# Block-sparse attention and a rational FFN on one core: the first batch's keys stay in SBUF for all its parts, and GpSimd copies the sampled blocks

## The chip, the cores and the metric

One core of a Trainium2 chip runs the whole program. The metric is device time in microseconds (us) of one launch. Inputs come from the chip's memory (DRAM in the code) and the output goes back there. The engines are TensorE (PE in the profile), VectorE (DVE), ScalarE (ACT), GpSimd (POOL) and SyncE (SP), which issues nearly all DMA transfers. Each engine works through its own queue in order.

## The reference

Shapes: `q`, `k`, `v` are 4 batches x 8 heads x 768 positions x 64, in float32. Positions form 24 blocks of 32. `sampled_blocks` names three key blocks for each query block.

```
scores = scale * q @ k^T
mask: |query block - key block| <= 1, or either block is 0 or 23,
      or the key block is one of the three sampled for the query block
attn = softmax(where(mask, scores, -1e9)); attn_out = attn @ v
x = attn_out as 3072 tokens x 512
h = x @ w_in                          (512 x 2048)
P = a0 + a1 h + a2 h^2 + a3 h^3;  Q = 1 + |b0||h| + |b1| h^2
out = (P / (Q + 1e-6)) @ w_out        (2048 x 512)
```

`w_in` and `w_out` arrive as 64-bit floats, and the kernel unpacks them itself.

## The kernel before

**Attention.** The work is cut into parts, a query block of 32 rows each with all eight heads. An ordinary query block needs eight key blocks: itself and its two neighbours, three sampled ones (3 to 5 in the tile) and blocks 0 and 23 (6 and 7). Query blocks 0 and 23 need all 24 key blocks and are cut into three parts of eight (`n` is 3 for those, 1 otherwise). A batch thus has 22 + 6 = 28 parts, in the order that `block(j)` gives: blocks 1 to 11, block 0, blocks 12 to 22, block 23. A part goes through scores (TensorE, L869), maxima with a bias that masks doubled blocks (VectorE, L879), the exponentials (ScalarE, L892), transposes (L935), a copy of these to SBUF, and the product with the values in tile `vg` (L992), which come from DRAM for each part.

**Keys.** `prep` loads a batch's keys, finds a scale, splits them into f16 high and low halves and transposes them. For batch 0 the transposed keys land in `kall`, which holds all 24 blocks (12 KB in each partition). For later batches they land in `kt` and are stored to a DRAM tile `ks`. From `ks` each part loads its eight key blocks into a slot: one transfer for the neighbours, at times one for blocks 0 and 23 (`fresh`), and one for each sampled block, at a row that SP reads from the table `ix` into registers (`sampled_rows`, L768).

**The near parts.** Batch 0's keys are also stored to `ks`. Its first eight parts (`near`, `x < KX`, `KX = CB = 8`) use `kall` itself: VectorE reads the sampled rows into its registers and copies the three blocks to `kx`, and the scores take three pieces: neighbours (96 columns), `kx` (96), blocks 0 and 23 (64). All other parts of batch 0 load from `ks` like those of later batches. Their slots are the three thirds of `kall`, which become free when the near parts are done with it.

**FFN.** Tokens are cut into 12 chunks of 256 (three to a batch), and each chunk into eight units of 256 hidden columns: matmuls with `w_in` in high and low halves (L1090 to L1092), the rational function on ScalarE and VectorE, and matmuls with `w_out` (L1146 to L1148). Ahead of that, weights are loaded to `wl`, unpacked by VectorE (L434, L437, L440), and split by ScalarE and GpSimd: `w_in` through the two buffers `ws`, `w_out` through the two buffers `dw`. Early in the program the attention of batch 0, the preparation of batch 1, this unpacking and the first units run interleaved.

**The order.** Each piece of work is an `Op` with an engine, a price in ns, a priority `prio`, and the ring slots that it takes and uses. `issue` is a planner: it simulates the engines with these prices (a transfer costs its issue, 650 ns, its bytes at 360 bytes per ns, and 900 ns), and repeatedly emits the operation that can start first, priority deciding ties. The emitted order is then fixed in each engine's queue. Until its own clock reaches 80 us, the planner also emits dummy matmuls (`fill`, L159) where TensorE would be idle. So a change of an operation's engine or price can move later work to other places in the queues, too.

**The pool switch.** The tiles of `early` (weight unpacking, `kx`) are freed at one point (`switch`), after the last weight is unpacked, the last `kx` copy and the first chunk's input. Their memory then serves four more `ld` buffers and a fourth key slot, `xkg`.

Of the kernel before, what the change touches and what calls it, by code (L numbers as in the profile page):

```python
# [11 lines left out]
F32 = mybir.dt.float32  # L12
F32R = mybir.dt.float32r
F16 = mybir.dt.float16
I32 = mybir.dt.int32
# [8 lines left out]
def kernel(  # L24
# [27 lines left out]
    nc = tc.nc  # L52
    B, H, S, D = q.shape
    DM, DFF = out.shape[1], w_out.shape[0]
    P = 128
    BLK = 32
    NB = S // BLK
# [215 lines left out]
    r_ld, r_hl, r_kt = Ring([p3] * 3), Ring([None] * 2), Ring([None])  # L273
    r_ldq, r_hlq, r_qa, r_fc, r_ks = Ring([None]), Ring([None]), Ring([None] * 2), Ring([None] * 2), Ring([None] * 2)
    r_cq, r_scq, r_xn = Ring([None] * 4), Ring([None] * 3), Ring([None])
    r_wl, r_dw, r_ws, r_kx, r_sums = Ring([None] * 2), Ring([None] * 2), Ring([None] * 2), Ring([None] * 2), Ring([None] * 2)


    sb32 = sampled_blocks.bitcast(I32).rearrange("(o i) n -> o (i n)", o=1)
# [107 lines left out]
    WC = 512  # L387
# [13 lines left out]
    def weights():  # L401

        wi64, wo64 = w_in.bitcast(I32), w_out.bitcast(I32)
        pieces = []
        for u in range(NG):
            pieces += [(min(place[0, 2 * u], place[1, 2 * u]) + -4.91, 0, u, x) for x in range(NCC)]
        for x in range(NF):
            pieces.append((min(place[0, x // 2], place[1, x // 2]) + x % 2 / 2 + 0.45, 1, x // NCC, x))  # L410
        pieces.sort(key=lambda p: p[0])
        sums, before = {}, None

        def one(prio, kind, u, x, before):
            d = {}
            s_wl = Slot(r_wl)
            s_w = Slot(r_dw) if kind else None

            def load():
                d["ld"] = early.tile([P, 2 * WC], I32, name="wl", bufs=2)  # L420
                if kind:
                    nc.sync.dma_start(out=d["ld"], in_=wo64[x * P:(x + 1) * P])
                    return
                for g in range(2):
                    nc.sync.dma_start(out=d["ld"][g * D:(g + 1) * D], in_=wi64[(g * HG + x) * D:(g * HG + x + 1) * D, u * 2 * WC:(u + 1) * 2 * WC])

            def convert(eng):
                d["w"] = early.tile([P, WC], I32, name="dw") if kind else wi[:, x, u].rearrange("p a n -> p (a n)").bitcast(I32)
                d["words"] = d["ld"].rearrange("p (n w) -> p n w", w=2)
                times(eng, d["w"].bitcast(F32), d["words"][:, :, 1].bitcast(F32), 2.0 ** -112)  # L430

            def pack1():
                w = d["w"]
                nc.vector.tensor_scalar(out=w, in0=w, scalar1=3, scalar2=None, op0=ALU.logical_shift_left)  # L434

            def pack2():
                nc.vector.scalar_tensor_tensor(out=d["w"], in0=d["words"][:, :, 0], scalar=29, in1=d["w"], op0=ALU.logical_shift_right, op1=ALU.bitwise_or)  # L437

            def pack3():
                nc.vector.scalar_tensor_tensor(out=d["w"], in0=d["words"][:, :, 1], scalar=-2 ** 31, in1=d["w"], op0=ALU.bitwise_and, op1=ALU.bitwise_or)  # L440

            def most():
                if u not in sums:
                    sums[u] = early.tile([P, 8], F32, name="sums")
                bound(d["w"].bitcast(F32), sums[u][:, x:x + 1])

            def out_high(eng):
                times(eng, wo_h[:, x], d["w"].bitcast(F32), 1.0)

            def out_low(eng):  # L450
                eng.tensor_tensor(out=wo_l[:, x], in0=d["w"].bitcast(F32), in1=wo_h[:, x].bitcast(F32), op=ALU.subtract)  # L451

            o0 = Op(SY, [(475, 524288)] if kind else [(475, 262144)] * 2, load, (), prio - 2, takes=[s_wl], behind=before)
            w = [s_w] if kind else []
            o = Op(among("c", SC, sc=520, po=588, ve=335), 0, convert, [o0], prio, takes=w, uses=[s_wl])
            o = Op(VE, 335, pack1, [o], prio, uses=w)
            o = Op(VE, 602, pack2, [o], prio, uses=[s_wl] + w)
            o = Op(VE, 602, pack3, [o], prio, uses=[s_wl] + w)
            if kind:
                o1 = Op(among("o", SC, sc=520, po=588, ve=335), 0, out_high, [o], prio, uses=w)  # L460
                o2 = Op(among("p", PO, po=1225, ve=602), 0, out_low, [o1], prio, uses=w)
                out_ready[x] = [o2]
                decoded.append(o2)
                return o0, o2
            return o0, Op(SC, 613, most, [o], prio)

        group = []
        for prio, kind, u, x in pieces:
            before, o = one(prio, kind, u, x, before)
            if kind == 0:  # L470
                group.append(o)
                if x == NCC - 1:
                    group = w_scaled(u, prio, group, sums) or []

    def w_scaled(u, prio, group, sums):
# [9 lines left out]
        scale_ready[u] = o  # L485
        for x in range(NCC):
            def three(x):
                d, s_ws = {}, Slot(r_ws)

                def scaled(eng):  # L490
                    d["w"] = early.tile([P, WC], F32, name="ws")
                    times(eng, d["w"], wi[:, x, u].rearrange("p a n -> p (a n)").bitcast(F32), sc[0])

                def high(eng):
                    times(eng, wi[:, x, u, 0], d["w"], 1.0)

                def low(eng):
                    eng.tensor_tensor(out=wi[:, x, u, 1], in0=d["w"], in1=wi[:, x, u, 0], op=ALU.subtract)

                a = Op(among("s", PO, po=671, ve=396, sc=613), 0, scaled, [o], prio, takes=[s_ws])  # L500
                a = Op(among("h", SC, sc=520, po=588, ve=335), 0, high, [a], prio, uses=[s_ws])
                a = Op(among("l", PO, po=1113, ve=602), 0, low, [a], prio, uses=[s_ws])
                in_ready.setdefault(u, []).append(a)
                decoded.append(a)
            three(x)
# [109 lines left out]
    def rest(b, w, j, d, o_scale, sc, prio, before):  # L615
# [63 lines left out]
        a.behind = k_evac[b, t][0] if g else None  # L679
        c = Op(among("e", VE if on_dve[1] else SC, sc=478, ve=598), 0, evac(1), [o, a], prio, uses=[s_ps, sk])  # L680
        k_evac.setdefault((b, t), []).extend([a, c])
        if g == 1:
            k_done[b].append(Op(SY, [(475, 524288)], store, k_evac[b, t], prio + (13.03 if first else 0), uses=[sk, s_scr[b]]))

    k_evac = {}

# [93 lines left out]
        has[kind, slot.buf] = b if n == 1 else None  # L780
        return old != b

    KX = CB

    def v_plain(buf):

# [8 lines left out]
    def attention(b, j, prio):  # L795
# [11 lines left out]
        for m, x in enumerate(xs):  # L807
            def one(m, x):
# [3 lines left out]
                deps = [Q["oq"], Q["oc"]]  # L812
                kslots = []
                h = {}
                if near:
                    s_kx = Slot(r_kx)

                    def copies():
                        rows = sampled_rows(x, mybir.EngineType.DVE)
                        h["kx"] = early.tile([P, NR, H, BLK], F16, name="kx")  # L820
                        for r in range(NR):
                            o_, i_ = h["kx"][:, r].rearrange("p h r -> p (h r)"), kall[:, bass.ds(rows[r], 1)].rearrange("p o h r -> p (o h r)")
                            nc.vector.tensor_copy(out=o_, in_=i_)

                    a = Op(VE, 470, copies, [o_setup] + [o for t in range(NCH) for o in k_evac[b, t]], p - 1, takes=[s_kx], uses=s_kall)
                    deps.append(a)
                    kslots = [s_kx] + s_kall
                    last_copies.append(a)
                else:
                    s_kg = Slot(r_kg)  # L830

# [25 lines left out]
                def scores():  # L857
                    qa, qc = Q["q"]
                    h["sp"] = sp = ps_s.tile([P, 512], F32, name="sp").rearrange("p (g n) -> p g n", g=2)
                    spv = sp.rearrange("p g (s r) -> p g s r", r=BLK)  # L860
                    if near:
                        pieces = [(slice(0, 3), kall[:, i - 1:i + 2]), (slice(3, 3 + NR), h["kx"]), (slice(3 + NR, NS), kall[:, 0:NB:NB - 1])]
                    else:
                        pieces = [(slice(0, NS), kgs[s_kg.buf])]
                    for g in range(2):
# [9 lines left out]
                def maxima():  # L875
                    st = d["st"]
                    add = bias[:, i] if n == 1 else bias[:, 0, 0:1].broadcast_to([P, NS])
                    for g in range(2):
# [2 lines left out]
                            in1=add.rearrange("p (s o) -> p s o", o=1).broadcast_to([P, NS, BLK]),  # L881
                            op0=ALU.add, op1=ALU.max, scale=1.0, scalar=-3.0e38, accum_out=st[:, 2 * m + g:2 * m + g + 1])

                o = chain["sc"] = Op(TE, 1010 if near else 668, scores, deps, p, behind=chain.get("sc"), takes=[s_sp, s_pr] + ([s_st] if m == 0 else []),
                                     uses=kslots + [Q["slot"]] + ([] if m == 0 else [s_st]))
                o.work = 0.4 if near else 1.0
                omax.append(Op(VE, 690, maxima, [o, o_setup], p, uses=[s_sp, s_pr, s_st]))

                def exps():
# [158 lines left out]
        l = Op(VE, 602, evac_low, [a], p, uses=[s_ps, s_xs[c]])  # L1048
        o_ready.setdefault(c, []).append(l)

    last_copies = []
    XB = 4
    x_group = {}

# [176 lines left out]
        return lambda w, stage, j: p0 - A[stage] + (w * 6 + j) * (([0.5, 0.5] if b == 1 else [0.85, 0.83])[stage])  # L1231

    prep(0, when(0))
    weights()
    before = None
    for b in range(B):
# [17 lines left out]
    def switch():  # L1254
        early_cm.__exit__(None, None, None)
        ext.append(ctx.enter_context(tc.tile_pool(name="ext", bufs=1)))
        t = max(o.end for o in decoded)
        r_ld.free += [(t, ext[0])] * 4
        for j in range(1):
            kgs.append(ext[0].tile([P, NS, H, BLK], F16, name=f"xkg{j}"))  # L1260
            r_kg.free.append((t, len(kgs) - 1))

    Op(None, 0, switch, decoded + last_copies + o_ready[0], -1)
    ctx.enter_context(tc.manual_schedule(engines={getattr(mybir.EngineType, n) for n in (TE, SC, VE, PO, SY)}))
    issue(8)

# [28 lines left out]
```

## Time and profile before

| | |
|---|---|
| median of 3 runs | 916.02 us (915.13 to 920.15) |
| the profiled execution | 923.66 us, its span 921.9 us |
| TensorE, VectorE, ScalarE, GpSimd busy | 836.3, 760.6, 649.5, 125.2 us |
| mean granted TensorE clock | 0.959 |
| DMA traffic | 159.04 MB in 261124 packets, mean 173 GB/s |

The span runs from the first to the last instruction of one execution taken by the profiler. "Busy" is the time in which an engine executes. A row of the forty slices has one digit for each 23 us, the busy share in tenths. In a table of stretches, the columns are the limits, the length, each engine's busy time with its count of instructions, the granted clock, the mean share in which the 16 DMA engines were busy, and GB/s. A row of waits names who waited for whom, the total, how often, and the longest. A row of transfers gives the destination and source, the queue, the count, the size of each and the median time from issue to landing. A row of a timeline has start, duration, engine, line, operation and, in brackets, idle time ahead of it.

### The profile page before, as it was taken

What the parts mean: (1) busy time and instruction counts of PE and PEld (TensorE: products, weight loads), DVE (VectorE), ACT (ScalarE), POOL (GpSimd) and SP (SyncE); (2) the same over time, 40 slices, a digit from 0 to 9 for tenths busy, and PEclk for the clock granted to TensorE, in tenths of its full rate; (3) what the DMA queues carried; (4) which work ended last, traced back from release to release, by engine and by line L of the source; (5) the groups of instructions that cost most, each with busy time, mean ns of one, the idle gap of its engine ahead of it and who ended that gap; (6) DMA issues with size and microseconds to landing.
All of it is one profiled execution on the core that took longest, in us unless ns stands there. A gap on an engine that the chain in (4) does not pass through costs nothing.

```text
span 921.9 us, 27328 instructions
## 1 busy us (share of the span) xinstructions
PE 836.3 (91%) x10214; PEld 646.7 (70%) x10214; DVE 760.6 (83%) x2065; ACT 649.5 (70%) x1373; POOL 125.2 (14%) x125
## 2 busy tenths in 40 slices
PE   7798876578889989989999999989999999999997
PEld 3365554356668768768888777768877787788886
DVE  5667986899999778787888788779878988877886
ACT  6476664776868677768776788687777777767663
POOL 2123621345420000020000000110000000000000
PEclk9988997789999999999999999999999999999999
DMA  8889899999875896677756976677656566541000
GB/s 221 199 182 237 210 230 205 199 227 248 243 178 151 216 252 172 162 175 196 191 145 175 226 211 167 162 195 204 161 142 171 145 170 166 157 113 47 1 24 23
DMA packets 261124, 159.04 MB, mean 173 GB/s; under 512 B 17152, under 2 KB 245376, under 8 KB 260992
## 3 DMA queue, kind: packets, MB, share of 16 engines
q1 hardware_dynamic: 260992, 157.30, 68.4%
q8 instruction: 81, 1.33, 0.6%
q14 instruction: 51, 0.42, 0.2%
HBM read 138.36 MB, written 12.58 MB: 164 GB/s over the span
## 4 chain that ended last, share of the span: by engine, by line
PE 56%; DMA 13%; DVE 12%; SPq 5%; issue 4%; ACT 4%; POOL 1%; DVEq 0%; ACTq 0%; POOLq 0%
PE acc L1146 7%; PE ph L1090 7%; PE acc L1148 7%; PE acc L1147 7%; PE ph L1091 6%; PE ph L1092 6%; PE av L992 5%; PE sp L869 4%; PE pt L935 4%; DMA vg<-in_v_dram 3%; DMA ld<-in_k_dram 2%; DMA ldq<-in_q_dram 2%; DMA wl<-in_moe_w_in_dram 2%; DMA ks<-kt 1%; DMA kall<-ks 1%
## 5 line engine op out<-in xcount | busy, mean ns | idle before, releaser
L1090 PE MATMUL ph<-xh,wi 128*128 128x256 f16 x768 | 212.8, 277 | 2.0 <-DVE tt L1107 2.0
L1091 PE MATMUL ph<-xl,wi 128*128 128x256 f16 x768 | 211.5, 275 | 0.0
L1092 PE MATMUL ph<-xh,wi 128*128 128x256 f16 x768 | 211.3, 275 | 0.0
L1146 PE MATMUL acc<-wo_h,gh 128*128 128x512 f32 x384 | 164.2, 428 | 3.8 <-ACT ld L147 2.5
L1148 PE MATMUL acc<-wo_h,gl 128*128 128x512 f32 x384 | 154.3, 402 | 4.8 <-DVE gl L1135 4.8
L892 ACT ACTIVATE pr<-pr,st,cq 128x256 f32<-128x256 f32 x224 | 132.1, 593 | 36.3 <-DVE st L903 36.2
L1147 PE MATMUL acc<-wo_l,gh 128*128 128x512 f32 x384 | 153.7, 400 | 1.1 <-POOL wo_l L451 1.1
L1097 ACT ACTIVATE sq<-ph,fc 128x512 f32<-128x512 f32 x96 | 65.5, 682 | 77.8 <-PE ph L1092 77.6
L1114 DVE SCALAR_TENSOR_TENSOR ab<-sq,absb,ab 128x512 f32<-128x512 f32 x96 | 73.4, 765 | 35.9 <-ACT ab L1111 35.6
L1090 PEld LDWEIGHTS <-wi 128*128 128x128 f16 x768 | 76.0, 99 | 31.1 <-issue 18.3
L879 DVE CUSTOM_DVE_ANT_1 pr<-sp,bias 128x256 f32<-128x256 f32 x224 | 84.8, 418 | 14.7 <-PE sp L869 14.2
L992 PE MATMUL av<-vg,pT 128*32 128x64 f32 x3584 | 76.1, 228 | 21.8 <-DMA vg<-in_v_dram 14.3
L992 PEld LDWEIGHTS av<-vg,pT 128*32 128x32 f32 x3584 | 58.2, 113 | 48.4 <-issue 16.7
L1148 PEld LDWEIGHTS acc<-wo_h,gl 128*128 128x128 f32 x384 | 73.5, 191 | 24.1 <-DVE gl L1135 6.5
L151 POOL TENSOR_SCALAR hlq<-ldq,scq 128x512 f16<-128x512 f32 x24 | 24.4, 1016 | 481.9 <-DVE scq L352 292.2
L1146 PEld LDWEIGHTS acc<-wo_h,gh 128*128 128x128 f32 x384 | 73.5, 191 | 21.4 <-ACT ld L147 3.0
L935 PE MATMUL pt<-ident,pr 128*128 128x128 f32 x448 | 78.6, 297 | 8.3 <-ACT pr L892 7.7
L1147 PEld LDWEIGHTS acc<-wo_l,gh 128*128 128x128 f32 x384 | 73.8, 192 | 13.9 <-POOL wo_l L451 1.4
L1092 PEld LDWEIGHTS <-wi 128*128 128x128 f16 x768 | 75.9, 99 | 9.5
L1091 PEld LDWEIGHTS <-wi 128*128 128x128 f16 x768 | 76.0, 99 | 9.2 <-issue 1.2
L1125 DVE SCALAR_TENSOR_TENSOR gh<-tt,par,rr 128x512 fp32r<-128x512 f32 x96 | 74.5, 776 | 8.5 <-PE acc L1147 7.1
L935 PEld LDWEIGHTS pt<-ident,pr 128*128 128x128 f32 x448 | 67.1, 207 | 20.0 <-ACT pr L892 10.4
(138 smaller groups left out, 1663.7 us busy)
## 6 DMA issues: line engine op xcount, KB each, us to landing
vg<-in_v_dram SPq DMA_DIRECT2D x312, 64.0 KB, 3.3
vg<-in_v_dram SPq DMA_DIRECT2D x88, 192.0 KB, 4.2
vg<-in_v_dram SPq DMA_DIRECT2D x24, 512.0 KB, 4.8
kall<-ks SPq DMA_DIRECT2D x63, 192.0 KB, 3.7
kall<-ks SPq DMA_DIRECT2D x189, 64.0 KB, 2.5
kall<-ks SPq DMA_DIRECT2D x21, 512.0 KB, 6.3
ld<-in_k_dram SPq DMA_DIRECT2D x36, 256.0 KB, 5.4
wl<-in_moe_w_in_dram SPq DMA_DIRECT2D x32, 256.0 KB, 4.5
```

The lines of the kernel that those rows point to most:

```text
L879: nc.vector.tensor_tensor_reduce(out=prs[x][:, g].rearrange("p (s r) -> p s r", r=BLK), in0=h["sp"][:, g].rearrange("p (s r) -> p s r", r= ...
L892: nc.scalar.activation(out=prs[x][:, g], in_=prs[x][:, g], func=AF.Exp, scale=Q["c"], bias=st[:, 6 + g:7 + g], accum_out=st[:, 8 + 2 * m + ...
L935: nc.tensor.transpose(pp[:, jj * P:(jj + 1) * P], cols, ident)
L992: nc.tensor.matmul(av[rows, g], pT[:, 2 * g + kt, rows] if plain else pT[:, 2 * g + kt, pa_, rows], vf[:, g * HG + h4, kt * D:(kt + 1) * D ...
L1090: nc.tensor.matmul(o, wh, xh[:, :, cc], start=(cc == 0), stop=False)
L1091: nc.tensor.matmul(o, wh, xl[:, :, cc], start=False, stop=False)
L1092: nc.tensor.matmul(o, wl, xh[:, :, cc], start=False, stop=(cc == NCC - 1))
L1114: nc.vector.scalar_tensor_tensor(out=d["ab"], in0=d["sq"], scalar=absb[:, 1:2], in1=d["ab"], op0=ALU.mult, op1=ALU.add)
L1125: nc.vector.scalar_tensor_tensor(out=d["gh"], in0=d["tt"], scalar=par[:, 0:1], in1=d["rr"], op0=ALU.add, op1=ALU.mult)
L1146: nc.tensor.matmul(acc[:, t], ghs, wo_h[:, f], start=(new and e == 0), stop=False)
L1147: nc.tensor.matmul(acc[:, t], ghs, wo_l[:, f], start=False, stop=False)
L1148: nc.tensor.matmul(acc[:, t], gls, wo_h[:, f], start=False, stop=(last and e == 1))
```

## The change

All 28 parts of batch 0 are now near (`KX` counts them), and batch 0's keys are no longer stored to `ks` nor loaded from it. The six parts with `n > 1` use the thirds of `kall` as they are, in one piece, without a copy. For the 22 others GpSimd reads the sampled rows into its registers and copies the three blocks into one of the two buffers of a fixed tile, `kxs`. That tile also holds blocks 0 and 23, which GpSimd copies once into each buffer (`edges`), so that the scores take two pieces (96 and 160 columns). The rings of `ws` and `dw` become one of three buffers. The pool switch waits for the last near scores in place of the last copy and the first chunk's input.

```
-    r_wl, r_dw, r_ws, r_kx, r_sums = Ring([None] * 2), Ring([None] * 2), Ring([None] * 2), Ring([None] * 2), Ring([None] * 2)
+    r_wl, r_dw, r_kx, r_sums = Ring([None] * 2), Ring([None] * 3), Ring(range(2)), Ring([None] * 2)
...
-                d["w"] = early.tile([P, WC], I32, name="dw") if kind else ...
+                d["w"] = early.tile([P, WC], I32, name="dw", bufs=3) if kind else ...
...
-                d, s_ws = {}, Slot(r_ws)
+                d, s_ws = {}, Slot(r_dw)
...
-                    d["w"] = early.tile([P, WC], F32, name="ws")
+                    d["w"] = early.tile([P, WC], I32, name="dw", bufs=3).bitcast(F32)
...
-        if g == 1:
-            k_done[b].append(Op(SY, [(475, 524288)], store, k_evac[b, t], prio + (13.03 if first else 0), uses=[sk, s_scr[b]]))
+        if g == 1 and not first:
+            k_done[b].append(Op(SY, [(475, 524288)], store, k_evac[b, t], prio, uses=[sk, s_scr[b]]))
...
-    KX = CB
+    KX = sum(1 for p in parts if p[0] == 0)
+    kxs = early.tile([P, 2, NR + 2, H, BLK], F16, name="kx", bufs=1)
...
-                if near:
+                if near and n > 1:
+                    deps += [o for t in range(NCH) for o in k_evac[b, t]]
+                    kslots = s_kall
+                elif near:
                     s_kx = Slot(r_kx)
 
                     def copies():
-                        rows = sampled_rows(x, mybir.EngineType.DVE)
-                        h["kx"] = early.tile([P, NR, H, BLK], F16, name="kx")
+                        rows = sampled_rows(x, mybir.EngineType.Pool)
                         for r in range(NR):
-                            o_, i_ = h["kx"][:, r]..., kall[:, bass.ds(rows[r], 1)]...
-                            nc.vector.tensor_copy(out=o_, in_=i_)
-
-                    a = Op(VE, 470, copies, [o_setup] + [o for t in range(NCH) for o in k_evac[b, t]], p - 1, takes=[s_kx], uses=s_kall)
+                            nc.gpsimd.tensor_copy(out=kxs[:, s_kx.buf, r]..., in_=kall[:, bass.ds(rows[r], 1)]...)
+
+                    a = Op(PO, 1500, copies, [o_setup, chain["edges"]], p - 1, takes=[s_kx], uses=s_kall)
                     deps.append(a)
                     kslots = [s_kx] + s_kall
-                    last_copies.append(a)
...
-                    if near:
-                        pieces = [(slice(0, 3), kall[:, i - 1:i + 2]), (slice(3, 3 + NR), h["kx"]), (slice(3 + NR, NS), kall[:, 0:NB:NB - 1])]
+                    if near and n > 1:
+                        pieces = [(slice(0, NS), kgs[m])]
+                    elif near:
+                        pieces = [(slice(0, 3), kall[:, i - 1:i + 2]), (slice(3, NS), kxs[:, s_kx.buf])]
...
-                o = chain["sc"] = Op(TE, 1010 if near else 668, scores, ...
+                o = chain["sc"] = Op(TE, 800 if near else 668, scores, ...
...
+                if near:
+                    last_near.append(o)
...
+    def edges():
+        for e in range(2):
+            nc.gpsimd.tensor_copy(out=kxs[:, e, NR:]..., in_=kall[:, 0:NB:NB - 1]...)
...
+    chain["edges"] = Op(PO, 1400, edges, [o for t in range(NCH) for o in k_evac[0, t]], -40, uses=s_kall)
...
-        t = max(o.end for o in decoded)
+        t = max(o.end for o in decoded + last_near)
...
-    Op(None, 0, switch, decoded + last_copies + o_ready[0], -1)
+    Op(None, 0, switch, decoded + last_near, -1)
```

More of the change, by code (lines that the diff above doesn't have):

```diff
@@ L427, in convert @@
             def convert(eng):
-                d["w"] = early.tile([P, WC], I32, name="dw") if kind else wi[:, x, u].rearrange("p a n -> p (a n)").bitcast(I32)
+                d["w"] = early.tile([P, WC], I32, name="dw", bufs=3) if kind else wi[:, x, u].rearrange("p a n -> p (a n)").bitcast(I32)
                 d["words"] = d["ld"].rearrange("p (n w) -> p n w", w=2)
@@ L814, in one @@
                 h = {}
-                if near:
+                if near and n > 1:
+                    deps += [o for t in range(NCH) for o in k_evac[b, t]]
+                    kslots = s_kall
+                elif near:
                     s_kx = Slot(r_kx)
                     def copies():
-                        rows = sampled_rows(x, mybir.EngineType.DVE)
-                        h["kx"] = early.tile([P, NR, H, BLK], F16, name="kx")
+                        rows = sampled_rows(x, mybir.EngineType.Pool)
                         for r in range(NR):
-                            o_, i_ = h["kx"][:, r].rearrange("p h r -> p (h r)"), kall[:, bass.ds(rows[r], 1)].rearrange("p o h r -> p (o h r)")
-                            nc.vector.tensor_copy(out=o_, in_=i_)
-                    a = Op(VE, 470, copies, [o_setup] + [o for t in range(NCH) for o in k_evac[b, t]], p - 1, takes=[s_kx], uses=s_kall)
+                            nc.gpsimd.tensor_copy(out=kxs[:, s_kx.buf, r].rearrange("p h r -> p (h r)"), in_=kall[:, bass.ds(rows[r], 1)].rearrange("p o h r -> p (o h r)"))
+                    a = Op(PO, 1500, copies, [o_setup, chain["edges"]], p - 1, takes=[s_kx], uses=s_kall)
                     deps.append(a)
                     kslots = [s_kx] + s_kall
-                    last_copies.append(a)
                 else:
@@ L882, in maxima @@
                             op0=ALU.add, op1=ALU.max, scale=1.0, scalar=-3.0e38, accum_out=st[:, 2 * m + g:2 * m + g + 1])
-                o = chain["sc"] = Op(TE, 1010 if near else 668, scores, deps, p, behind=chain.get("sc"), takes=[s_sp, s_pr] + ([s_st] if m == 0 else []),
+                o = chain["sc"] = Op(TE, 800 if near else 668, scores, deps, p, behind=chain.get("sc"), takes=[s_sp, s_pr] + ([s_st] if m == 0 else []),
                                      uses=kslots + [Q["slot"]] + ([] if m == 0 else [s_st]))
                 o.work = 0.4 if near else 1.0
+                if near:
+                    last_near.append(o)
                 omax.append(Op(VE, 690, maxima, [o, o_setup], p, uses=[s_sp, s_pr, s_st]))
@@ L1049, in attention @@
         o_ready.setdefault(c, []).append(l)
-    last_copies = []
+    def edges():
+        for e in range(2):
+            nc.gpsimd.tensor_copy(out=kxs[:, e, NR:].rearrange("p s h r -> p s (h r)"), in_=kall[:, 0:NB:NB - 1].rearrange("p s h r -> p s (h r)"))
+    last_near = []
     XB = 4
```

## The prediction

> **What bounds the kernel now.** I read the page's forty slices of the span first, for where TensorE is idle.
>
> ```profile
> span 921.9 us, 27328 instructions
> ...
> PE   7798876578889989989999999989999999999997
> ...
> DMA  8889899999875896677756976677656566541000
> ```
>
> From slice 12 on (about 260 us) TensorE is nearly always busy; before it, it isn't, and there the DMA row stands at 8 and 9. The question is what limits the first 260 us, so next I cut them into stretches: up to the first reload of the first batch's keys, the reloads, up to the first scores of batch 1 in full flow, and the rest.
>
> ```profile
> core 0: us, PE busy (x) PEld busy (x) DVE busy (x) ACT busy (x) POOL busy (x), PEclk, DMA share, GB/s
> 26.00:71.00 45.00, 36.67 (x774) 23.03 (x772) 29.54 (x141) 26.18 (x67) 8.78 (x11) 0.89 0.90 200
> 71.00:215.00 144.00, 103.24 (x1205) 72.00 (x1204) 122.61 (x314) 94.13 (x206) 55.46 (x50) 0.85 0.99 219
> 215.00:262.00 47.00, 38.02 (x458) 28.49 (x459) 45.49 (x99) 33.71 (x73) 22.63 (x20) 0.94 0.85 238
> ...
> 260.00:922.00 662.00, 640.46 (x7695) 515.40 (x7694) 549.62 (x1467) 480.93 (x996) 32.82 (x31) 0.99 0.60 155
> ```
>
> In 71 to 215 the DMA engines are 99% busy, and TensorE (72%), VectorE (85%) and ScalarE (65%) all have room: the DMA is the limit. In 215 to 262 VectorE is (45.49 of 47). After 260 TensorE is (640.46 of 662), so a stretch saved ahead of 260 moves the end by as much. The waits of 71 to 215 say the same: weights and values come late, and GpSimd, ScalarE and TensorE stand for them.
>
> ```profile
> POOL dw L151 <- DMA wl<-in_moe_w_out_dram: 31.9, 4, 23.5
> ...
> ACT wi L147 <- DMA wl<-in_moe_w_in_dram: 15.7, 8, 3.3
> PE av L992 <- DMA vg<-in_v_dram: 13.0, 6, 6.7
> ...
> PE sp L869 <- DMA kall<-ks: 4.8, 4, 3.0
> ```
>
> **The reloads go (71 to 215).** What the keys of batch 0 cost there is in the list of transfers of that stretch:
>
> ```profile
> DMA packets 44320, 31.49 MB, mean 219 GB/s; under 512 B 2948, under 2 KB 41048, under 8 KB 44302
> ...
> kall<-ks SPq DMA_DIRECT2D x6, 512.0 KB, 6.8
> ...
> kall<-ks SPq DMA_DIRECT2D x14, 192.0 KB, 4.9
> kall<-ks SPq DMA_DIRECT2D x42, 64.0 KB, 3.8
> ...
> kall<-ks SPq DMA_DIRECT2D x6, 128.0 KB, 4.2
> ```
>
> 6x512 + 14x192 + 42x64 + 6x128 = 9216 KB, 9.44 MB of 31.49. At 219 GB/s that is 43 us of transfer time and 68 issues on SP's queue; all of it goes. The other 22.05 MB need 101 us of 144: the DMA no longer limits. Register loads of the sampled rows stay on SP, which still needs them for the values. TensorE's 4.8 us for keys go too, but what is late next is VectorE. It has 122.61 us of work in the 144. How tightly can it be packed? 96.8% in 215 to 262; a little less while the DMA was still full:
>
> ```profile
> 80.00:100.00 20.00, 17.06 (x179) 10.62 (x178) 17.92 (x52) 14.40 (x31) 11.34 (x13) 0.85 1.09 243
> 100.00:120.00 20.00, 17.18 (x262) 12.26 (x261) 19.17 (x48) 14.64 (x36) 9.32 (x7) 1.00 0.85 226
> ```
>
> 37.09 of 40, 92.7%.
>
> **The copies on GpSimd.** Fourteen parts with three copies each land in this stretch, 42 copies of 128x256 f16 with none of that size on GpSimd in the trace. The nearest rows on both sides are 128x128 and 128x512:
>
> ```profile
> 1.08 0.29 POOL masks.py:199 TENSOR_SCALAR_AFFINE_SELECT ident<-ident 128x128 f32<-128x128 f32 x1
> ...
> 61.88 0.67 POOL L151 TENSOR_SCALAR wi<-wl 128x512 f32<-128x512 f32 x1 [3.04 <-DMA wl<-in_moe_w_in_dram]
> ```
>
> 0.29 to 0.67; a third of the way between them in elements gives 0.41 us, which I take: 17.2 us beside GpSimd's 55.46 in 144. That engine has room, but VectorE slows when GpSimd runs:
>
> ```profile
> 123.79 0.66 POOL L151 TENSOR_SCALAR dw<-wl 128x512 f32<-128x512 f32 x1 [1.37 <-DMA wl<-in_moe_w_out_dram]
> ...
> 129.75 1.52 POOL L451 TENSOR_TENSOR wo_l<-dw,wo_h 128x512 fp32r<-128x512 f32 x1
> ...
> 130.06 1.75 DVE L1128 SCALAR_TENSOR_TENSOR ab<-ab,gh 128x512 f32<-128x512 f32 x1
> ...
> L440 DVE SCALAR_TENSOR_TENSOR wi<-wl,wi 128x512 int32<-128x512 int32 x11 | 8.7, 789 | 0.1
> L440 DVE SCALAR_TENSOR_TENSOR dw<-wl,dw 128x512 int32<-128x512 int32 x9 | 7.9, 883 | 0.0
> L437 DVE SCALAR_TENSOR_TENSOR dw<-wl,dw 128x512 int32<-128x512 int32 x9 | 7.9, 879 | 0.0
> L437 DVE SCALAR_TENSOR_TENSOR wi<-wl,wi 128x512 int32<-128x512 int32 x11 | 7.5, 686 | 0.1
> ```
>
> L1128 began inside the GpSimd instruction and ended 0.54 us after it. The four groups below are one shape; against 686 ns they lose 11x0.10 + 9x0.20 + 9x0.19 = 4.6 us. Other instructions with two inputs were stretched like L1128, and I double it: 9 us for 55 of GpSimd, 0.17 per us; with 0.2, the copies cost VectorE 3.4 us. The Trainium skill (SBUF — State Buffer, section "SBUF: two separate sides") says that VectorE with two SBUF inputs and a GpSimd instruction hold one port pair as an exclusive lock, the later one waiting to the other's end. The 1.75 us of L1128 agree; by that rule alone the copies could cost up to their own 17.2 us (first rival).
>
> VectorE's need becomes 126.0 us. At 96.8% that takes 130.2 us (13.8 saved), at 92.7% 135.9 (8.1). Both are stages of the same work, so I take 11. The ends: at today's 85.1% it would take 148.1 (4 lost), fully packed without the stretch 122.6 (21 saved).
>
> **The first eight parts (26 to 71).** The store of the keys goes, and the sampled copies leave VectorE.
>
> ```profile
> DMA packets 10920, 9.01 MB, mean 200 GB/s; under 512 B 859, under 2 KB 9429, under 8 KB 10911
> ...
> ks<-kall SPq DMA_DIRECT2D x3, 512.0 KB
> ...
> L768 DVEq TENSOR_LOAD <-ix x8: 743/746/2016, 27.2 to 51.8; - x8
> ...
> L823 DVE COPY kx<-kall 128x256 f16 x24 | 4.0, 222 | 5.8 <-issue 5.0 <-PE sp L869 0.8
> ...
> L823 DVE COPY kx<-kall x24: 218/220/229, 29.4 to 53.0; 128x256 f16 x24
> ```
>
> 1.57 MB at 200 GB/s are 7.9 us of transfers; VectorE gets back 4.0 us of copies and 5.0 of idle behind register loads. GpSimd gets, per part, a register load (0.75 as on VectorE) and three copies at 0.41, some 2.0 us, eight times, and two edge copies of 128x512 by 0.67: 17 us beside 8.78 in 45. The parts now come every 3.4 us (copies from 29.4 to 53.0, seven steps), so GpSimd keeps up, with two buffers. But the first part waits for 1.3 + 0.75 + 1.2 = 3.3 us in place of 0.75 + 3x0.22 = 1.4, which TensorE fills with dummy work. Neither VectorE (29.54 of 45) nor GpSimd limits here; the DMA at 0.90 does in part. Ends: 8 saved (all the transfer time), 3 lost (a late first part, and GpSimd late again once); I take 2 saved.
>
> **Scores.** A far part issues four groups of four 256-wide matmuls 0.11 us apart; a near one now eight groups, 96 and 160 wide:
>
> ```profile
> 122.86 0.29 PE L869 MATMUL sp<-kall,qa 128*32 128x256 f16 x4
> 122.97 0.30 PE L869 MATMUL sp<-kall,qc 128*32 128x256 f16 x4
> ...
> 30.11 0.23 PE L869 MATMUL sp<-kall,qa 128*32 128x96 f16 x4
> 30.15 0.23 PE L869 MATMUL sp<-kall,qc 128*32 128x96 f16 x4
> ```
>
> 4x0.11 against 4x0.04 + 4x0.07: nothing either way, up to 1 us for 14 parts; idle TensorE hides it, and at full speed it would cost that 1.
>
> **The shared dw ring** (three buffers for two pairs): a dw buffer lives from its first to its last instruction, 123.79 to 131.27 above, 7.5 us; a ws buffer, with three steps for six, about half. 16 of each are some 180 buffer-us against 3x144 = 432 in that stretch alone: nothing, hidden by the free buffers; without them, one wait of some 4 us.
>
> **Batch 1.** All three key slots come free only with batch 0's last scores, and the extra pool also waits for them:
>
> ```profile
> 234.22 0.30 PE L869 MATMUL sp<-kall,qc 128*32 128x256 f16 x4
> ...
> 237.62 0.45 SPq L838 DMA_DIRECT2D kall<-ks  x1
> ...
> L451 POOL TENSOR_TENSOR wo_l<-dw,wo_h x16: 1254/1286/2733, 92.7 to 261.1; 128x512 fp32r<-128x512 f32 x16
> ```
>
> The first load is already issued 3.4 us after that point, and the pool waits till 261 for decoding. Nothing, as long as both move together. Past 260 only the written-out order changes: 0, with 3 us either way.
>
> **Sum:** 11 + 2 = 13 us off the profiled execution. That one took 923.66 us with a span of 921.9, 0.8% over the median of 916.02. 910.7 x 916.02/923.66 = 903; I say 903.
>
> **The rivals.**
> *Hidden by VectorE.* If each us of copies stops VectorE for a us, its need is 139.8, at 96.8% 144.4 us: nothing saved, and with the first stretch 914. For it: L1128 above, and VectorE's 85%. Against: 55 us of GpSimd have cost it nearer 9 than 55.
> *GpSimd's queue holds the scores (slower).* A copy stands in order behind GpSimd instructions that wait for weights: 31.9 us in four waits, the longest 23.5. The scores behind it stand, and on TensorE everything behind those. With two buffers a copy can be two parts ahead, about 14 us in this stretch, which covers the three short waits (8.4 together) but not 23.5. If the wait of 23.5 stays and short ones find no lead, three stalls of about 8 us, 24 in all, take the 13 and give 11 more: 927. It decides from 13 us of such stalls. Against: those waits are for transfers, which now come earlier.
> *Batch 1's keys late.* If its loads lag 10 us behind the last scores, attention of batch 1 starts 10 later, TensorE has other units meanwhile, and half shows: 908 on top of the gain, 921 without it.
>
> **How the numbers follow.** The forecast 0.68, the first rival 0.17, GpSimd's queue 0.11, the late keys without a gain 0.04. A measurement of this kernel tells 0.5% (4.6 us) from no change: faster 0.68, same 0.17, slower 0.15. The range goes from 890 (21 and 5 saved, scaled) to 920, which leaves out the slower cases and little below.
>
> **What would show it.** Right: no `ks` transfers for batch 0; DMA share in the stretch of the reloads near 0.8; waits for vg and wl below half; VectorE over 93%; the last wo_l near 248 instead of 261. Wrong: GpSimd's copies over 0.6 us, VectorE's two-input instructions near 1 us, TensorE waiting for GpSimd's copies ahead of scores, GpSimd's copies waiting long for scores of two parts before, or the startup ending where it does now.

## The result, and the profile after

The changed kernel took 903.01 us (median of 4 runs, 898.97 to 905.26) against 917.38 before: ratio 0.9836, 95% interval [0.9801, 0.9871]. A second series gave 0.9856 [0.9827, 0.9884]. The forecast was 903. The profiled execution of before (923.66 us) lies above its median and that of after (898.97 us) below, so they differ by more than the medians; where time is counted below, the ratios count, and the profiles serve for where it went. The ratios leave out slow runs, of which there was one: 1576.46 us, of the kernel below that makes the copies on VectorE.

The page after, and its three stretches, with the same limits and columns as before:

```profile
span 897.2 us, 27426 instructions
...
PE   6879868576899999989999999989999999999997
...
DMA  8889686467966987688666986787756566740000
```

```profile
26.00:71.00 45.00, 36.80 (x652) 20.78 (x650) 33.82 (x134) 30.63 (x77) 24.80 (x44) 0.92 0.83 186
71.00:215.00 144.00, 109.34 (x1536) 79.66 (x1536) 130.24 (x326) 102.65 (x219) 77.68 (x87) 0.89 0.68 169
215.00:262.00 47.00, 39.20 (x523) 30.62 (x521) 45.48 (x114) 32.73 (x72) 14.01 (x11) 0.93 0.87 220
```

In the stretch of the reloads the DMA share fell from 0.99 to 0.68. VectorE does 7.6 us more work in the same 144 us (130.24 against 122.61), ScalarE 8.5, TensorE 6.1. VectorE is at 90%. The waits for weights and values in that stretch shrank from 31.9, 15.7 and 13.0 us to:

```profile
POOL dw L151 <- DMA wl<-in_moe_w_out_dram: 6.5, 1, 6.5
...
ACT wi L147 <- DMA wl<-in_moe_w_in_dram: 5.2, 4, 2.1
...
PE av L997 <- DMA vg<-in_v_dram: 4.1, 1, 4.1
```

One view that the prediction doesn't use is the waits of SP's own queue in 71 to 215. First the kernel before, its longest:

```profile
SPq L843 <- DMA kall<-ks: 1.9, 1, 1.9
SPq L843 <- DMA vg<-in_v_dram: 1.7, 4, 0.6
SPq L836 <- PE sp L869: 1.7, 1, 1.7
```

and after:

```profile
SPq L422 <- DVE wi L440: 9.1, 4, 4.9
SPq L961 <- PE av L997: 7.7, 3, 4.6
SPq L422 <- DVE dw L440: 7.0, 3, 3.5
SPq L703 <- DVE st L908: 7.0, 1, 7.0
```

Added up over all rows of that view, SP stood 20.5 us before, of which 14 for an earlier transfer to land and 1.1 for VectorE; after, it stood 71 us, 47.8 of them for VectorE to free a buffer. Before, SP seldom waited for work: by its timeline it issued 184 transfers, which took 107.6 of the 144 us (118 and 72.7 us after), and its register loads come on top. A piece of it (start, duration, and the next issue hard behind it):

```profile
123.28 1.73 SPq L425 DMA_DIRECT2D wl<-in_moe_w_in_dram  x2
125.10 0.54 SPq L956 DMA_DIRECT2D vg<-in_v_dram  x1
125.69 0.46 SPq L958 DMA_DIRECT2D vg<-in_v_dram  x1
126.20 0.42 SPq L959 DMA_DIRECT2D vg<-in_v_dram  x1
126.82 1.33 SPq L962 DMA_DIRECT2D vg<-in_v_dram  x3
```

So the stretch had two resources that were nearly always in use, the DMA engines and SP's queue, and the change relieved both. They are not independent: 14 of SP's 20.5 us of waiting were for transfers. Which of them paid is what the experiments ask.

### The profile page after: what moved, and what is told of

The parts are those of the page before. It is cut to its first block, busy times and chain, and to the rows that moved or that the text cites. A ratio compares the mean times of both kernels' runs of the same rounds, so it can differ in the third digit from the quotient of the medians.

```text
span 897.2 us, 27426 instructions
## 1 busy us (share of the span) xinstructions
PE 824.4 (92%) x10310; PEld 640.1 (71%) x10310; DVE 760.5 (85%) x2042; ACT 652.7 (73%) x1380; POOL 152.1 (17%) x185
## 4 chain that ended last, share of the span: by engine, by line
PE 66%; DVE 12%; DMA 9%; ACT 7%; SPq 3%; issue 2%; POOL 0%; ACTq 0%; POOLq 0%; DVEq 0%
PE acc L1155 8%; PE ph L1099 8%; PE acc L1157 8%; PE acc L1156 8%; PE ph L1101 7%; PE ph L1100 7%; PE av L997 6%; PE pt L940 5%; PE sp L872 4%; DMA wl<-in_moe_w_in_dram 2%; ACT pr L897 2%; PE acc L159 1%; DMA ld<-in_k_dram 1%; DVE pr L882 1%; DMA ks<-kt 1%
## 5 line engine op out<-in xcount | busy, mean ns | idle before, releaser
L147 ACT ACTIVATE pT<-pt 128x512 f32<-128x512 f32 x112 | 66.6, 594 | 18.1 <-PE pt L940 17.3
```

## The experiments

All ratios are to the kernel before, run beside them. The theory was: the bytes of the reloads are the gain, and VectorE is next. The rivals: the planner's new order; SP's queue; the copies that left VectorE.

**The bytes alone, in the order of before.** Most keys of batch 0's late parts are left stale.

```
+ cut = 8 if b == 0 else P;  flat = flat[:cut]
- nc.sync.dma_start(out=flat[:, 0:3], in_=ks[i - 1:i + 2]...)
+ nc.sync.dma_start(out=flat[:, 0:3], in_=ks[i - 1:i + 2, :cut]...)      (and so for every reload)
```

> The kernel before, with nothing changed but the bytes of batch 0's key reloads: each of the 68 transfers moves 8 of the 128 partitions, so most of the keys of those parts are stale. Queues, order, waits and VectorE's copies stay. If the freed transfer time is the gain (theory): 9.44 MB fall to 0.59, DMA share in the stretch of the reloads from 0.99 to about 0.75, ratio to before 0.984 to 0.990 (9 to 14 us off). If the gain came from the planner's new order, from SP's shorter queue or from the copies that left VectorE: 0.997 to 1.003.

Measured: 0.9941 [0.9917, 0.9965], 5.4 us of the 13 to 15: less than the theory expected, more than the rivals. The bytes pay, but less than half. In the stretch VectorE and TensorE got through as much as in the changed kernel (130.24 and 109.34), so what this run lacks of the gain must show elsewhere:

```profile
71.00:215.00 144.00, 109.13 (x1329) 78.34 (x1327) 131.40 (x328) 100.48 (x220) 62.63 (x56) 0.88 0.77 180
```

**The same bytes in fewer transfers, in the order of before.** The keys are wrong here, blocks 0 to 5 or 0 to 7 for every ordinary part of batch 0.

```
+ if b == 0:
+     z = NS if h["new"] else 3 + NR
+     nc.sync.dma_start(out=flat[:, 0:z], in_=ks[0:z]...)
+     return
```

> The kernel before, with the same bytes of key reloads for batch 0 but one transfer of six or eight neighbouring blocks for each ordinary part, instead of four or five (wrong keys: blocks 0 to 5 or 0 to 7 for all): 48 issues fewer, some 20 us of SP. If SP's issues are the other half of the gain: ratio 0.990 to 0.996. If the bytes are all of it: 0.998 to 1.002.

Measured: 0.9960 [0.9937, 0.9984], 3.7 us off, at the edge of what was expected, though the DMA engines were as full as before:

```profile
71.00:215.00 144.00, 106.90 (x1255) 75.55 (x1253) 123.28 (x320) 97.02 (x211) 59.01 (x53) 0.85 1.02 228
```

48 transfers fewer pay by themselves. SP's queue is no longer full here: by the same tally it stands 55.1 us in place of 20.5. Whether the gain comes by SP's issue time, by fewer landings to wait for, or by larger transfers moving a little faster (228 GB/s against 219), this run doesn't tell apart.

**Both cuts together.**

```
+ nc.sync.dma_start(out=flat[:, 0:z], in_=ks[0:z, :cut]...)
```

> The kernel before, with the two single cuts together: batch 0's key reloads move 8 of 128 partitions, and an ordinary part issues one transfer instead of four or five (most keys of those parts are stale or wrong). Order, copies and waits of before. If bytes (5 us alone) and issues (4 us alone) are two halves of the gain and add up: ratio 0.986 to 0.992, 8 to 12 us off. If either one alone frees the same time: 0.993 to 0.996. What is left to 0.984 would be the new order and the waits for slots.

Measured: 0.9913 [0.9891, 0.9935], 8.0 us; the two single runs add up to 9.1. The interval lies below that of the fewer transfers alone, but it overlaps that of the bytes alone: that the count of transfers still pays once the bytes are gone isn't shown. In the stretch the two profiles agree (VectorE 132.04 and 131.40, TensorE 109.79 and 109.13). SP now waits for VectorE, as it does after the change:

```profile
SPq L422 <- DVE wi L440: 12.1, 4, 4.5
SPq L425 <- DVE dw L440: 7.3, 3, 3.3
```

The reloads, bytes and transfers, are thus 8 us of the gain. From 0.9913 to 0.9856, beside which it ran, another 5 us remain; they come from what this kernel keeps: the early store, the waits of reloads for slots, the copies on VectorE, and the old order. They were not separated further, except for the next run.

The profiles show where much of that rest may lie: behind the startup, from 300 to 340 us. Here are the kernel before, the one with both cuts, and the changed kernel in its two series:

```profile
300.00:340.00 40.00, 35.26 (x437) 28.15 (x436) 30.75 (x86) 29.52 (x68) 1.22 (x1) 0.98 0.95 242
300.00:340.00 40.00, 34.54 (x410) 27.51 (x408) 29.38 (x85) 27.68 (x63) 1.22 (x1) 0.96 1.00 255
300.00:340.00 40.00, 40.00 (x513) 32.63 (x513) 35.14 (x97) 32.50 (x74) 1.18 (x1) 1.00 0.89 237
300.00:340.00 40.00, 39.91 (x489) 32.28 (x488) 35.58 (x101) 31.41 (x74) 1.18 (x1) 1.00 0.91 246
```

TensorE stands 4.7 us before and 5.5 us with both cuts, most of it for ScalarE's exponentials and the copies behind them, and at most 0.1 us after. From 260 to 400 us it works 132.74 of 140 us with both cuts, 135.19 and 138.78 after.

```profile
PE pt L935 <- ACT pr L892: 3.6, 1, 3.6
PE av L992 <- ACT pT L147: 1.1, 2, 0.8
```

That is read from single executions and not tested, and which part of the change removes this stall is open. The granted clock is no part of the remaining 5 us: averaged over the runs of that series it was 0.967 with both cuts and after the change alike. Before, it was 0.961; no run tells whether that is a cause of some of the 8 us or follows from fewer stalls.

**The copies alone.** The first eight parts as in the change, the reloads and the store as before.

```
- KX = sum(1 for p in parts if p[0] == 0)
+ KX = CB
- if g == 1 and not first:
+ if g == 1:                       (the store of batch 0 again)
```

> One part of the change alone: the first eight parts' copies on GpSimd with the fixed tile, the edges and the shared ring, but the other parts of batch 0 reload their keys from DRAM as before, and the store of the keys stays. Theory (the reloads are the gain): ratio 0.997 to 1.003, since VectorE's 9 us lie in a stretch where it has room. Rival (VectorE's copies were a good part of the gain): 0.993 or less.

Measured: 0.9980 [0.9952, 1.0009]. Moving the copies off VectorE, with the edges and the shared ring, is no measurable gain or loss by itself.

**The transfers put back into the changed kernel, read by nobody.**

```
+ if near and x >= CB:             (in scores; jk is scratch in DRAM)
+     nc.sync.dma_start(out=jk..., in_=kall...)    68 in all: 6 x 512, 14 x 192, 42 x 64, 6 x 128 KB
```

> The kernel after, with 68 transfers of the same sizes put back beside each late part of batch 0, from the resident keys to scratch memory that nobody reads; nobody waits for them and the planner does not know them. Theory (bytes): the gain is mostly given back, ratio 0.992 to 1.002, waits for vg and wl return. Rival (order, engines): stays at 0.984, at most 2 us more for SP's issues.

> As the one before, but each of the 68 transfers moves 8 of 128 partitions: SP's issue time without the bytes. Theory: 0.984 to 0.988, as after. If SP's queue was the limit: 0.992 and more, as with the full bytes.

Measured: 1.0077 [1.0049, 1.0104] with the bytes, 0.9952 [0.9929, 0.9975] with 8 of 128 partitions. Both expectations missed. The first is even slower than before: these transfers stand in SP's queue where the planner knew of none, and weights come later behind them (ScalarE's waits for `w_in` in the stretch are 14.9 us, after the change 5.2). The second should have stayed at 0.984, and lost 9 to 11 us with a sixteenth of the bytes; its waits for `w_in` are 12.0 us. SP's longest waits there for a transfer are on the added ones:

```profile
SPq L870 <- DMA wl<-in_moe_w_out_dram: 4.0, 4, 1.2
```

Here issues of 4 KB stand until an earlier transfer has landed. And although the edit gives nobody a reason to wait for them, one wait of TensorE for values (4.8 us) is put down to the landing of an added transfer. This run is what pointed to the count of transfers, but the places of the added ones count in it too.

**SP's time without transfers.**

```
+ rows_of[x, eng] = [load of one value for r in range(NR)]    in place of one load of three, 14 parts
```

> The kernel after, with the sampled rows of 14 late parts of batch 0 read into SP's registers by three loads of one value each instead of one load of three: 28 more loads at 0.67 us, 19 us of SP's time with no bytes and no transfers. If SP's time was a limit beside the bytes (what the run with tiny transfers points to): 4 us and more over after, 0.988 to 0.994. If that run lost its time by something else (its transfers' places, waits for their landing): 0.983 to 0.986.

Measured: 0.9880 [0.9844, 0.9917], median 904.48 us. The interval holds parts of both answers. And the edit did not add the 19 us: a load of one value takes 0.27 us, not the 0.67 of a load of three.

```profile
L768 SPq TENSOR_LOAD <-ix x42: 260/270/297, 66.2 to 189.9; - x42
```

42 of these against 14 at 0.675 us are 1.9 us more of SP's time, where SP has 71 us of waits in that stretch. So this run says nothing on SP's time as a limit.

**VectorE as the next limit.**

```
- rows = sampled_rows(x, mybir.EngineType.Pool); nc.gpsimd.tensor_copy(...)
+ rows = sampled_rows(x, mybir.EngineType.DVE);  nc.vector.tensor_copy(...)
- Op(PO, 1500, copies, ...)
+ Op(VE, 470, copies, ...)
```

> The kernel after, with the register loads and the three copies of each part on VectorE instead of GpSimd (66 copies at 0.22 us, 22 register loads at 0.75 us, 31 us of VectorE); the keys still stay in SBUF. Theory (VectorE is next once the DMA is relieved): 14 parts in the stretch cost 14 x 1.4 = 20 us of VectorE there, most of it seen, and the gain is gone: ratio 0.994 to 1.006. Rival (VectorE has room, the gain is the transfers alone): 0.983 to 0.988.

Measured: 0.9904 [0.9866, 0.9942]. Neither answer: 4 to 6 us of the 20 show, with an interval that touches those of the changed kernel. First the stretch, then its copies alone (VectorE's busy time, count, then clock, DMA share and GB/s):

```profile
71.00:215.00 144.00, 100.14 (x1369) 72.60 (x1366) 130.76 (x357) 99.22 (x215) 60.80 (x54) 0.85 0.70 171
71.00:215.00 144.00, 11.19 (x36) 0.85 0.70 171
```

VectorE is busy as long as after the change (130.24), and 11.19 us of it are copies. So the stretch holds 10.7 us less of VectorE's other work than after the change: the copies displaced it nearly us for us. In every kernel here that takes the reloads' bytes away and puts no transfers back, VectorE is busy 90 to 92% of the stretch. That fits a limit, with waits of its own in the rest; why no more than 4 to 6 us show at the end, the run doesn't tell.

**What GpSimd costs VectorE.**

```
+ for _ in range(2):
      nc.gpsimd.tensor_copy(out=kxs[...], in_=kall[...])
```

> The kernel after, with each of the 66 copies made twice: 26 us more of GpSimd. If GpSimd costs VectorE 0.2 us for each us as in the trace of before: 3 to 5 us more than after, ratio 0.986 to 0.990. If its copies stop VectorE one for one: 15 us and more, ratio 0.999 or more.

Measured: 0.9942 [0.9913, 0.9971], 8 to 10 us over the changed kernel: between the two answers, and twice what 0.2 us per us gives. VectorE's instructions are the same in both kernels, so how much they were stretched can be read from its busy time, first the changed kernel, then this one:

```profile
PE 824.4 (92%) x10310; PEld 640.1 (71%) x10310; DVE 760.5 (85%) x2042; ACT 652.7 (73%) x1380; POOL 152.1 (17%) x185
```

```profile
PE 829.4 (91%) x10310; PEld 642.2 (71%) x10310; DVE 766.5 (85%) x2042; ACT 653.4 (72%) x1380; POOL 190.3 (21%) x251
```

VectorE has 6.0 us more (in the second series of the changed kernel it has 760.6, so that is clear of the noise). GpSimd's copies are, again in this order, and with the mean of one in ns:

```profile
L825 POOL COPY kx<-kall 128x256 f16 x66 | 33.3, 545 | 14.6 <-PE sp L872 14.0 <-POOL wi L151 0.3 <-POOL hlq L151 0.2
L826 POOL COPY kx<-kall 128x256 f16 x132 | 67.8, 532 | 13.0 <-PE sp L873 4.7 <-issue 4.1
```

The 66 more copies took 34.5 us, not 26, since the mean of one lies above the median of 0.40 us. 6.0 of 34.5 is 0.17 per us, as the prediction had it. Even if all 6 reach the end, 2 to 4 us have another source. GpSimd's queue is longer ahead of everything behind the copies; that was not separated. The exclusive lock that the Trainium skill states (SBUF — State Buffer, section "SBUF: two separate sides") gives a bound: had every copy stopped VectorE for its length, VectorE's busy time would have grown by 34, not 6.

**Two attempts at a faster version.** Four buffers of three blocks without edge copies:

```
- Ring(range(2)); kxs = early.tile([P, 2, NR + 2, H, BLK], ...); edges
+ Ring(range(4)); kxs = early.tile([P, 4, NR, H, BLK], ...); blocks 0 and 23 from kall
```

> The kernel after with four buffers of three sampled blocks instead of two buffers of five, blocks 0 and 23 read from the resident keys (three score pieces again), and no edge copies. GpSimd stood 14 us for scores of two parts before, and the edge copies ahead of the first part go. If those waits hold up the unpacking behind them: 2 to 5 us less than after, ratio 0.978 to 0.983. If VectorE is the limit all the same: as after.

Measured: 0.9835 [0.9812, 0.9858], median 902.58 us beside 903.93 of the changed kernel in the same series. The intervals overlap: not distinguishable. Copies on ScalarE:

```
+ rows = sampled_rows(x, mybir.EngineType.Activation); nc.scalar.activation(..., func=AF.Copy)
```

> The kernel after with register loads and sampled copies on ScalarE (22 x (0.75 + 3 x 0.4) = 43 us of ScalarE, some 27 in 71 to 215, where it has 41 free). GpSimd's copies stretch VectorE by some 4 to 6 us in all; if that and GpSimd's queue are what the copies cost, ratio 0.978 to 0.983. If ScalarE's queue now holds exponentials and splits behind the copies: slower than after, 0.986 to 0.996.

Measured: 0.9914 [0.9885, 0.9944], 5 us slower than the changed kernel. A copy costs 0.40 us there at the median, as on GpSimd, and none takes more than 0.43, where GpSimd's mean is 0.545. But the exponentials stand in the same queue: from 26 to 250 us ScalarE waits 19.5 us for the step ahead of them, where the changed kernel has 5.7. That this is the cause isn't shown.

```profile
L825 ACT ACTIVATE kx<-kall x66: 398/403/432, 29.1 to 211.4; 128x256 f16 x66
...
ACT pr L897 <- DVE st L908: 19.5, 11, 3.2
```

## Why the prediction was right, point by point

**The time** was right: 903 forecast, 903.0 and 903.9 measured. The sum was partly luck: the reloads are worth 8 us where it has 11, and all the rest 5 us where it has 2.

**The reloads go, 11 us.** The removal was as stated, no transfer of batch 0's keys is left. But the prediction gave the whole term to the bytes (43 us of transfer time) and counted the 68 issues without a price. The runs show 5.4 us for the bytes, 3.7 for 48 of the transfers, 8.0 for both. The step that failed is to take the bytes for the gain because "the DMA is the limit": with every issue in place the bytes gave half of the 11 us, and with the bytes in place fewer transfers paid too. The prediction shows no view of SP's queue. Whether the issues themselves were the second limit stays open.

**VectorE next, packed to between 92.7% and 96.8%.** It packs to 90.4%, below both, and the sign "VectorE over 93%" did not show. The test with the copies on VectorE shows that it takes on hardly any more work there, so 90 to 92% seems to be full for this stretch. The 8 us found with both cuts are at the lower of the two ends that were averaged.

**The copies at 0.41 us, the register loads at 0.75.** Measured, first the copies, then the loads, as minimum, median, maximum in ns:

```profile
L825 POOL COPY kx<-kall x66: 391/400/938, 30.9 to 201.2; 128x256 f16 x66
...
L768 POOLq TENSOR_LOAD <-ix x22: 726/731/941, 29.5 to 197.6; - x22
```

The median is right, but the mean of a copy is 0.545 us, a third over the 0.41 of the sum: the 36 copies that fall into the stretch took 20.2 us there, where the prediction has 17.2 for 42. The loads are right. The difference may be the same contention seen from GpSimd: its copies take up to 938 ns, while the same copies on ScalarE stay within 398 to 432. No run tests that.

**The first eight parts, 2 us.** The last of their scores starts at 51.59 in place of 56.14, the first whole part at 33.09 instead of 30.3:

```profile
33.09 0.24 PE L872 MATMUL sp<-kx,qc 128*32 128x160 f16 x4
...
51.59 0.26 PE L872 MATMUL sp<-kx,qc 128*32 128x160 f16 x4
```

A later start and a faster pace, as described. In 26 to 71 VectorE did 33.82 us of work, none of it copies; before, it did 29.54, and 3.98 of these were copies. So the gain there is larger than the 2 us in VectorE's work. That any of it reaches the end isn't shown: the copies alone gave 0.998 [0.995, 1.001], and the store alone was not tried.

**Past 260 (0 us, with 3 either way):** too small, as far as the profiles show. The stall of TensorE from 300 to 340 us, 4.7 us before, is gone. In the forty slices of before it is the 8 of the fifteenth slice, which the prediction's "nearly always busy" passes over.

**Hidden by VectorE (first rival):** excluded by the doubled copies, 0.17 us per us and not 1.

**GpSimd's queue holds the scores (second rival):** the queue does wait, but not as feared. Its longest waits in 71 to 215:

```profile
POOL kx L825 <- PE sp L872: 12.2, 4, 6.9
POOL wo_l L451 <- ACT wo_h L147: 9.4, 3, 7.9
POOL wo_h L151 <- DVE dw L440: 8.6, 3, 4.7
```

It is GpSimd that waits for scores, not the scores for GpSimd, and four buffers in place of two changed the time by nothing that can be measured. The waits for `w_out` went from 31.9 to 6.5 us, which was the argument against this rival.

**Batch 1's keys late (third rival):** the last wo_l starts at 250.5 us instead of 261.1, near the 248 that was named (255.0 in the second series), and TensorE is at 9 from the slice at 247 us on. One small sign of it: TensorE stands 3.3 us at 225 us for the first keys of batch 1, which it did not before.

```profile
L451 POOL TENSOR_TENSOR wo_l<-dw,wo_h x16: 1267/1463/1766, 79.9 to 250.5; 128x512 fp32r<-128x512 f32 x16
...
PE sp L872 <- DMA kall<-ks: 3.3, 1, 3.3
```

## What to carry to other kernels

Where the DMA engines are full, look at the issuing queue as well before pricing the bytes: if SP issues nearly all the time and waits mostly for earlier transfers, its count of transfers may be a second limit; here 48 fewer transfers of the same bytes paid 3.7 us. A resource at 99% does not make its relief worth its busy time: 43 us of transfers gone gave 5 us, and with most of their issues 8; the next engine was at 85% already and got no further than 90 to 92%. Moving the first eight parts' copies to an idle engine neither gained nor lost by itself. With the keys kept for all parts, GpSimd was the better place for the copies: on VectorE they cost 4 to 6 us more, on ScalarE 5. When a forecast comes true, check its terms one by one: here one was too large and the rest too small. A stage that seems full can hold a stall worth pricing: the 4.7 us from 300 to 340 us were counted as nothing.

## What the runs showed of the hardware that was not expected

Tiny transfers are not cheap when they are many and badly placed: 68 of 4 to 32 KB, 0.59 MB in all, cost 9 to 11 us in the changed kernel. The Trainium skill (DMA: Bandwidth & Descriptors, section "Issuing engines are not separate DMA queues") calls the time to initiate a transfer usually small relative to the transfer; here an issue takes about half a us (median 0.49 in 71 to 215 before) against 3.8 to 6.8 to land, by the medians of its groups, which agrees for one. But a queue that issues 184 in 144 us spends 107.6 us on it. GpSimd's copy of 128x256 f16 takes 0.40 us at the median and 0.545 on average beside a busy VectorE, ScalarE's 0.40, VectorE's 0.22 at the median. A register load of one value takes SP 0.27 us, of three 0.67.
